# A tuned attention and GLU kernel: phi = elu+1 as a minimum on VectorE in place of an add on GpSimd, a product in four tasks, smaller first loads and a smaller last store

## The chip, the cores and the metric

The kernel runs on one core of a Trainium2 chip. The metric is the device time of one execution in microseconds, the median of several runs. A profiled execution of the same kernel gives the trace; its times are measured from the start of the profiled span. Engines are PE (TensorE), DVE (VectorE), ACT (ScalarE), POOL (GpSimd) and SP (SyncE, which here issues DMAs).

## What is computed

x has 2048 rows of 512. Two branches share it, and a gate per row mixes them:

```
phi = lambda t: jnp.where(t > 0, t + 1.0, jnp.exp(t))
for s in range(N):                       # 4 segments of 512 rows, 32 heads of 16
    p = softmax(qs @ ks.T * scale + causal mask)
    a_dot = p @ vs
    a_mem = (phi(qs) @ M) / (phi(qs) @ z + 1e-6)
    o = g * a_mem + (1 - g) * a_dot      # g = sigmoid(beta), one per head
    M = M + phi(ks).T @ vs ; z = z + sum(phi(ks))
a = o @ wo
b = (gelu(x @ w_gate) * (x @ w_up)) @ w_down      # inner width 1792
out = g_row * a + (1 - g_row) * b        # g_row = sigmoid(x . gate_w)
```

phi(t) is elu(t) + 1. It can also be had as min(exp(t), 1) + max(t, 0), or as min(exp(t), max(t, 0) + 1).

## The kernel before, in words

Everything stays on the chip between loads and stores. PSUM has eight banks of 128x512 fp32, given out one at a time ("gen") or as pairs.

The program is written as tasks, each with an engine (or a choice of two), a cost in ns, dependences, a priority, and the banks and ring buffers that it takes and frees. `Sched.plan` simulates all engines with these costs and picks, engine by engine, the ready task of lowest priority number that can start first; `Sched.emit` then issues the instructions in that order. A random term of width SPREAD from the generator SEED is added to TensorE priorities, so SEED and SPREAD alter the whole order. The order in each engine's queue is fixed once the program is built: at run time an instruction waits for what it needs, and what stands behind it on its engine waits too. Tasks with `port=True`, and all tasks of POOL, are kept from overlapping in the plan.

**Opening** (`first_k`, L523 to L573). NWARM matmuls on zeros (L529) keep TensorE busy while x arrives. Rows 0 to 511 of x come as two DMAs of 256 KB, one issued by SP and one by ACT (L395), wk likewise (L397); the other weights follow on SP (L382 to L407), then the loads of the other segments of x, transposed by DMA (L377). Sixteen matmuls against the identity (L548), four for each block `fc` of 128 columns, transpose x; DVE and ACT in turn copy each block to xT (L552, through the helper at L314 and L316); then k is computed for all columns (L562), four matmuls for each `fc`. q, v and the gate projections follow (L475, full 128x128 tiles).

**Attention** runs from about 67 us. Each segment has 20 logit slots (L731): each computes two pairs of banks with row-tiled matmuls, ACT exponentiates them (L753), POOL zeroes the upper triangle of the diagonal blocks (L762), and after each five slots the P·V products follow (L781), whose results DVE transposes (L799), normalises (L809 to L817), joins with the memory part (L822) and transposes back into xT (L825). Between slots, as fillers, stand the dense products in column tiles (L479): q, k and v of the next segment, the up projections (evicted by DVE, L653), the memory products, and the down and output projections of the segment before. NUPS says how many of the 56 up projections each segment gets.

**phi** (L838 to L859) is done for two column groups at a time, 128x1024, twice per segment for k of segments 0 to 2 and for q of segments 1 to 3: twelve times. ACT writes E = exp(t) (L843), DVE writes Q = max(t, 0) (L847) and caps E at 1 in place (L850), and POOL adds the two (L854) into pkT or pq. pkT is transposed by a DMA issued on SP (L881), for the update of M (L892).

**M** is accumulated in Macc (L906, L908). At the end of each of the segments 0 to 2, `f_mbd` (L914) writes it as a block diagonal into Mbd with four products of 32 partitions, one task of 1000 ns in the plan; zbd (L920) likewise for z. The memory products of the next segment (L964) read Mbd.

**Output** (`out_group`, L999): for each 128 rows, 14 down and 4 output quads (four column tiles each) accumulate in one bank; DVE or ACT scales it into an osb buffer (two of them), and SP stores 128 KB (L997). The four groups of the last segment come last.

Of the kernel before, what the change touches and what calls it, by code (L numbers as in the profile page):

```python
# [9 lines left out]
AF = mybir.ActivationFunctionType  # L10
# [25 lines left out]
PORTPEN = 0  # L36
NWARM = 7
NUPS = (26, 12, 10, 8)
ATT = 5
SEED = 6  # L40
SPREAD = 3.0
SHAPES = {"gen": [(b,) for b in range(NBANK)],
# [246 lines left out]
def kernel(  # L289
# [22 lines left out]
    def copy(e, dst, src):  # L312
        if e == "ACT":
            nc.scalar.activation(dst, src, AF.Copy)  # L314
        else:
# [7 lines left out]
             "pkT": 1, "pk": 2, "T": 2, "r": 2, "N": 2, "rm": 1, "Tm": 1, "Nm": 3,  # L323
             "osb": 2, "tt": 1}
    S = Sched(RINGS)
# [67 lines left out]
    x0r = x2[0:L, :].rearrange("(kt p) d -> p kt d", p=P)  # L393
    for h, eng in enumerate((nc.sync, nc.scalar)):
        eng.dma_start(xn[:, 2 * h:2 * h + 2, :], x0r[:, 2 * h:2 * h + 2, :])  # L395
    for h, eng in enumerate((nc.sync, nc.scalar)):
        eng.dma_start(wk[:, 2 * h:2 * h + 2, :], wkr[:, 2 * h:2 * h + 2, :])  # L397
    load_w(nc.sync, wq, A_wq)
# [12 lines left out]

    a_xn = ext(3600)
    a_x = [None, ext(18000), ext(22000), ext(26000)]
    a_wk, a_wq = ext(3800), ext(5500)
    a_wg0, a_wv, a_wga, a_gw, a_be, a_wup, a_wo = [ext(t) for t in (8500, 10000, 14000, 27000,
# [85 lines left out]
    def qk_group(s, c, which, prio, engs):  # L501
        pr = c // 2
        W, aw = (wk, a_wk) if which == "k" else (wq, a_wq)
        key = (which, s, pr)
        name = which + "T"

        def mk():
            QK[key] = rtile(name, [P, 2, L])
        new = key not in first_ev
        g, box = group(which, 4 * MM, lambda t: mm_x(t[:, :], W, c * P, s), prio,  # L510
                       [a_x[s], aw] + ([] if new else [first_ev[key]]),
                       also=(name, mk) if new else None)
        first_ev.setdefault(key, g)
        read_x[s].append(g)

        def fn(e, t):
            copy(e, QK[key][:, c % 2, :], t[:, :])
        ev = evac(engs, g, box, fn)
        EVQK[(which, s, c)] = ev
        if which == "k":  # L520
            odd_copy(s, c, ev)

    def first_k():  # L523
# [8 lines left out]
        add("EXT", 0, lambda _: None, deps=[w], frees=[("pair", w)])  # L532

        def f_open(_):
            for i in range(2):
                tl["x", i] = pair(op, 0)[:, i, :]
                tl["x", 2 + i] = pair(op, 1)[:, i, :]
            for i in range(2):
                tl["k", i] = pair(op, 2 + i)
                QK[("k", 0, i)] = rtile("kT", [P, 2, L])  # L540
        op = add("PE", 1, f_open, prio=-2000, deps=[w], alloc=["pair", "pair", "pair", "pair", "kT",
                                                          "kT"])
        xe = []
        prev = op
        for fc in range(FC):
            def f_t(_, fc=fc):
                for kt in range(KT):
                    nc.tensor.matmul(tl["x", fc][:, kt * P:(kt + 1) * P],  # L548
                                     lhsT=xn[:, kt, fc * P:(fc + 1) * P], rhs=ident,
                                     start=True, stop=True)  # L550
            prev = add("PE", 430, f_t, prio=-1999, deps=[prev, a_xn])
            xe.append(add("ACT" if fc % 2 else "DVE", 600,  # L552
                          lambda e, fc=fc: copy(e, xT[:, fc, 0:L], tl["x", fc]), prio=0,
                          deps=[prev], frees=[(("pair", fc // 2), op)]))
        a_x[0] = xe[-1]
        TAB["wdn"] = add("SP", 600, lambda _: load_w(nc.sync, wdn, B_w_down), deps=[prev],
                         lat=40000)
        last = None
        for fc in range(FC):
            def fn(_, fc=fc):  # L560
                for c in range(NCH):
                    nc.tensor.matmul(tl["k", c // 2][:, c % 2, :],  # L562
                                     lhsT=wk[:, fc, c * P:(c + 1) * P], rhs=xT[:, fc, 0:L],
                                     start=(fc == 0), stop=(fc == FC - 1))
            last = add("PE", 4 * MM, fn, prio=-1998, deps=[last, xe[fc], a_wk])
            read_x[0].append(last)
# [271 lines left out]
    def phi(src, deps, prio, mk, ring):  # L838
        box = {}

        def f_e(_):
            box["E"] = rtile("E", [P, 2, L])
            nc.scalar.activation(box["E"][:, :, :], src()[:, :, :], AF.Exp)  # L843

        def f_q(_):
            box["Q"] = rtile("Q1", [P, 2, L])
            nc.vector.tensor_scalar_max(box["Q"][:, :, :], src()[:, :, :], 0.0)  # L847

        def f_m(_):
            nc.vector.tensor_scalar_min(box["E"][:, :, :], box["E"][:, :, :], 1.0)  # L850

        def f_a(_):
            d = mk()
            nc.gpsimd.tensor_add(d[:, :, :], box["E"][:, :, :], box["Q"][:, :, :])  # L854
        e = add("ACT", 960, f_e, prio=prio, deps=deps + [TAB["first_x"], opened], alloc=["E"])
        q = add("DVE", 325, f_q, port=True, prio=5, deps=[e], alloc=["Q1"])
        m = add("DVE", 330, f_m, port=True, prio=5, deps=[e])
        return add("POOL", 2090, f_a, prio=5, deps=[m, q], alloc=[ring],
                   frees=[("E", e), ("Q1", q)])  # L859
# [24 lines left out]
    def m_update(s, pr, prio):  # L884

        def mms(t):
            for i in range(2):
                for kt in range(KT):
                    for j in range(4):
# [8 lines left out]
                       [PKD[(s, pr)]] + [EVV[(s, kt)] for kt in range(KT)]  # L898
                       + ([TAB[("mbd", s - 1)], TAB[("zbd", s - 1)]] if s else []),
                       frees=[("pk", PKD[(s, pr)])])  # L900
# [12 lines left out]

        def f_mbd(_):  # L914
            for j in range(4):
                a, hh = slice(32 * j, 32 * j + 32), slice(2 * j, 2 * j + 2)
                nc.vector.tensor_mul(Mbd[a, :, hh, :], Macc[a, :, :, 0:DH], bdeb[a, :, hh, :])  # L917

# [7 lines left out]
        deps = [TAB[("acc", s, 0)], acc, t_eb] + [TAB[("num", s, c)] for c in range(NCH) if s]  # L926
        TAB[("mbd", s)] = add("DVE", 1000, f_mbd, port=True, prio=3, deps=deps)
        TAB[("zbd", s)] = add("DVE", 125, f_zbd, port=True, prio=3, deps=deps + ([TAB[("den", s)]] if s else []))
# [33 lines left out]
    def mem_num(s, c, prio):  # L962
        def mms(t):
# [3 lines left out]
        g, box = group("num", MM, mms, prio,  # L967
                       [TAB[("mbd", s - 1)], TAB[("den", s)], PHI[("q", s, c // 2)]],
                       also=("Tm", lambda: bx.update(T=rtile("Tm", [P, QB, 2, DH], F32))),
# [14 lines left out]

    def down(t, s, qt, lo, hi, stop):
        for hs in range(lo, hi):
            dense(t, G[:, s, hs, qt * P:(qt + 1) * P], wdn[:, hs, :], hs == 0,
                  stop and hs == HS - 1)

    def proj_o(t, s, qt, cs, first):  # L990
        for c in cs:
            dense(t, xT[:, c, s * L + qt * P:s * L + (qt + 1) * P], wo[:, c, :],
                  first and c == 0, c == NCH - 1)

    def store(s, qt, osb):
        q0 = s * L + qt * P
        nc.sync.dma_start(out2[q0:q0 + P, :], osb[:, :])  # L997

    def out_group(s, qt, prio):  # L999


        late = s == NSEG - 1
        att = [t_wo] + [OTT[(s, c)] for c in range(NCH)]
        prev = first = None
        for lo in range(0, HS, 2):
            def fn(_, lo=lo):
                down(bank(first), s, qt, lo, lo + 2, False)
            prev = add("PE", 2 * MM, fn, prio=prio, mode="more" if lo else "open",
                       deps=[prev] if lo else [UPT[(s, hs)] for hs in range(HS)] + [TAB["wdn"]]
                       + ([] if late else att[:ATT]), alloc=[] if lo else ["gen"], final=late)  # L1010
            first = first or prev
        g = add("PE", 4 * MM, lambda _: proj_o(bank(first), s, qt, range(NCH), False),
                prio=prio, deps=[prev] + att, final=late, mode="more")
        bx = {}

        def fo(e):
            bx["o"] = rtile("osb", [P, D])
            f = omz[:, s, qt:qt + 1]
            if e == "ACT":
                nc.scalar.activation(bx["o"][:, :], bank(first), AF.Copy, scale=f)  # L1020
            else:
                nc.vector.tensor_scalar_mul(bx["o"][:, :], bank(first), f)
        ev = add(["DVE", "ACT"], [660, 585], fo, deps=[g, TAB["omz"]], alloc=["osb"],
                 frees=[("gen", first)])
        add("SP", 600, lambda _: store(s, qt, bx["o"]), deps=[ev], frees=[("osb", ev)], lat=2000)

# [34 lines left out]
    for s in range(NSEG):  # L1061
        for t in range(NSLOT):
# [7 lines left out]
            if w == 4:  # L1070
                pv_group(s, c, 0)
                pv_group(s, c, 1)
    for qt in range(KT):
        out_group(NSEG - 1, qt, 9000 + qt)

    S.plan()
# [28 lines left out]
```

## Time and profile before

| what | us |
|---|---|
| median of 3 runs (lowest to highest) | 277.24 (277.02 to 277.30) |
| the profiled execution: its time | 277.76 |
| the profiled execution: its span | 275.93 |
| POOL's adds of phi, L854, 12 of them, each | 2.13 to 2.56 |
| POOL's selects L762: 96 of 128x512, 64 of 128x256, mean each | 0.67, 0.44 |
| DVE's cap L850, 12 of them, mean | 0.45 |
| ACT's exp of logits L753, 160 of them, mean (sum) | 1.03 (154.3) |
| stores of 128 KB, median from issue to landing | 2.1 |

The span is the time from the first to the last instruction in the trace; the execution's own time has some 1.8 us around it. A row of the timeline reads: start, duration, engine, line, operation, output<-inputs, shape, how many were merged, and in brackets how long the engine stood idle before and what released it. "128\*32" after PE is the active rows and columns of the array. A row of groups has busy time, the mean in ns, and the idle time before. A row of waits has the total in us, how many, and the longest. TensorE's matmuls are pipelined: a row of 0.38 us for a 128x512 matmul overlaps the next one, which starts 0.216 us later.

### The profile page before, as it was taken

How to read it: one execution, taken by the hardware profiler on the slowest of the kernel's cores; microseconds unless marked ns; L12 is line 12 of the kernel's file. 1: busy time of each engine (PE TensorE's matmuls, PEld its weight loads, DVE VectorE, ACT ScalarE, POOL GpSimd, SP SyncE). 2: the span in 40 equal slices, each digit the busy share in tenths (PEclk: the TensorE clock that was granted, in tenths of full speed). 3: DMA queues.
4: the chain of work that ended last, by engine and by line, in shares of the span. 5: the costliest groups of instructions: out<-in, count | busy, mean ns of one | idle time of the engine just before them, and what ended most of it. 6: DMA issues, size and time to landing. Idle time of an engine off the chain costs nothing.

```text
span 275.9 us, 10157 instructions
## 1 busy us (share of the span) xinstructions
PE 268.7 (97%) x4504; PEld 125.1 (45%) x4504; DVE 173.5 (63%) x323; ACT 211.6 (77%) x233; POOL 128.9 (47%) x221
## 2 busy tenths in 40 slices
PE   8999999999999979999999999999999999999994
PEld 4444444444444434544444444544444544444451
DVE  3340003001879898869778869999976795996240
ACT  3445555556987858799889799999988999999711
POOL 8100000070477356456844776676755457564500
PEclk9999999999999999999999999999999999999999
DMA  7963890000022000200110011020000000000002
GB/s 234 355 135 77 293 315 2 0 0 2 2 44 40 2 2 2 40 2 2 21 43 23 21 22 41 2 40 6 21 21 21 21 4 4 21 21 21 24 12 67
DMA packets 22036, 14.02 MB, mean 51 GB/s; under 512 B 14056, under 2 KB 20968, under 8 KB 21992
## 3 DMA queue, kind: packets, MB, share of 16 engines
q1 hardware_dynamic: 21448, 12.85, 16.8%
q8 instruction: 35, 0.57, 0.9%
q10 hardware_dynamic: 544, 0.52, 0.6%
q14 instruction: 9, 0.07, 0.1%
HBM read 8.13 MB, written 2.10 MB: 37 GB/s over the span
## 4 chain that ended last, share of the span: by engine, by line
PE 92%; DVE 4%; ACT 1%; issue 1%; ACTq 0%
PE ps L479 53%; PE ps L475 20%; PE ps L731 9%; PE ps L781 6%; PE ps L562 1%; PE ps L529 1%; DVE G L653 1%; ACT pT L753 1%; DVE Mbd L917 1%; PE ps L548 1%; DVE vz_82 L316 0%; DVE kT L316 0%; PE ps L892 0%; PE ps L597 0%; DVE E L850 0%
## 5 line engine op out<-in xcount | busy, mean ns | idle before, releaser
L753 ACT ACTIVATE pT<-ps 128x1024 bf16<-128x1024 f32 x160 | 154.3, 1029 | 15.4 <-PE ps L731 14.7
L762 POOL TENSOR_SCALAR_AFFINE_SELECT pT<-pT 128x512 bf16<-128x512 bf16 (+1 forms) x160 | 91.6, 579 | 80.4 <-ACT pT L753 80.0
L479 PE MATMUL ps<-wdn,G 128*32 128x512 bf16 x896 | 58.5, 380 | 0.0
L479 PE MATMUL ps<-xT,wup 128*32 128x512 bf16 x896 | 55.4, 380 | 0.1
L653 DVE TENSOR_TENSOR G<-ps,G 128x512 bf16<-128x512 f32 x56 | 37.9, 681 | 21.5 <-PE ps L479 21.4
L475 PE MATMUL ps<-xT,wga 128*128 128x512 bf16 x224 | 48.9, 379 | 0.0
L643 ACT ACTIVATE G<-ps 128x1024 bf16<-128x1024 f32 x28 | 28.7, 1024 | 23.5 <-PE ps L475 23.5
L799 DVE STREAM_TRANSPOSE T<-ps 128x512 f32<-128x512 f32 x32 | 22.7, 711 | 18.6 <-PE ps L781 15.1
L475 PEld LDWEIGHTS <-wga 128*128 128x128 bf16 x224 | 21.8, 98 | 26.4 <-issue 0.4
L479 PEld LDWEIGHTS <-wup 128*32 128x32 bf16 x896 | 22.3, 96 | 22.4 <-issue 4.0
L479 PEld LDWEIGHTS <-G 128*32 128x32 bf16 x896 | 21.4, 96 | 20.0 <-issue 2.7
L614 POOL COPY G_87<-tt 32x16 f32<-32x16 f32 x16 | 3.1, 195 | 48.2 <-DVE tt L606 47.6
L731 PE MATMUL ps<-qT,kO 32*128 32x128 bf16 (+2 forms) x320 | 17.9, 272 | 0.2 <-ACT pT L753 0.2
L731 PE MATMUL ps<-qT,kT 16*128 16x256 bf16 (+2 forms) x320 | 17.6, 274 | 0.0
L479 PEld LDWEIGHTS <-xT 128*32 128x32 bf16 x448 | 11.4, 96 | 12.6 <-issue 2.8
L479 PE MATMUL ps<-wo,xT 128*32 128x512 bf16 x256 | 16.3, 380 | 0.0
L731 PEld LDWEIGHTS <-kT 16*128 16x128 bf16 x320 | 6.8, 92 | 19.6 <-issue 19.5
L817 DVE TENSOR_TENSOR N<-T,r 128x512 bf16<-128x512 f32 x16 | 14.3, 893 | 0.3
L479 PE MATMUL ps<-wv,xT 128*32 128x512 bf16 x192 | 12.3, 380 | 1.6 <-DVE G L653 1.6
L731 PEld LDWEIGHTS <-kO 32*128 32x128 bf16 x320 | 7.1, 92 | 12.3 <-issue 12.1
L1020 ACT ACTIVATE osb<-ps,omz 128x512 bf16<-128x512 f32 x8 | 5.5, 689 | 9.3 <-PE ps L479 7.6
L479 PE MATMUL ps<-xT,wq 128*32 128x512 bf16 x192 | 12.3, 380 | 0.1
(117 smaller groups left out, 276.9 us busy)
## 6 DMA issues: line engine op xcount, KB each, us to landing
out_dram<-osb SPq DMA_DIRECT2D x16, 128.0 KB, 2.1
wup<-in_B_w_up_dram SPq DMA_DIRECT2D x1, 1792.0 KB, 8.2
wdn<-in_B_w_down_dram SPq DMA_DIRECT2D x1, 1792.0 KB, 13.7
wga<-in_B_w_gate_dram SPq DMA_DIRECT2D x1, 1280.0 KB, 10.9
wq<-in_A_wq_dram SPq DMA_DIRECT2D x1, 512.0 KB, 6.2
wga<-in_B_w_gate_dram SPq DMA_DIRECT2D x1, 512.0 KB
wv<-in_A_wv_dram SPq DMA_DIRECT2D x1, 512.0 KB, 8.2
wo<-in_A_wo_dram SPq DMA_DIRECT2D x1, 512.0 KB, 9.3
```

What stands on the lines that cost most here:

```text
L475: nc.tensor.matmul(t, lhsT=lhsT, rhs=rhs, start=start, stop=stop)
L479: nc.tensor.matmul(t[a, :], lhsT=lhsT[:, a], rhs=rhs, start=start, stop=stop, tile_position=(0, 32 * j), skip_group_check=True)
L614: nc.gpsimd.tensor_copy(G2[dst, s, :], z[src, :, 0])
L643: ge = evac("ACT", g, box, lambda e, t: nc.scalar.activation(dst, t[:, :, :], AF.Gelu_apprx_tanh), cost=920, ring="pair")
L653: UPT[(s, hs)] = evac("DVE", g, box, lambda e, t: nc.vector.tensor_mul(G[:, s, hs, :], t[:, :], G[:, s, hs, :]))
L731: nc.tensor.matmul(A[j // 2][:, j % 2, at * P:(at + nq) * P], lhsT=l, rhs=r, start=True, stop=True, tile_position=(32 * j, 0))
L753: nc.scalar.activation(pT[(s, t, h)][:, :, :], A[h][:, :, :], AF.Exp, scale=0.25)
L762: nc.gpsimd.affine_select(out=v, in_=v, pattern=pat, compare_op=ALU.is_ge, fill=0.0, base=0, channel_multiplier=-1)
L781: nc.tensor.matmul(t[32 * j:32 * j + 32, qb * P:(qb + nq) * P], lhsT=vz[s % 2][:, kt, h * VW:h * VW + 32], rhs=pT[(s, t0 + w, j // 2)][:, ...
L799: nc.vector.transpose(TT[key][:, e, :, :].rearrange("p a b -> p (a b)"), t[:, :])
L817: nc.vector.tensor_mul(NN[key][:, :, :, :].rearrange("p a e d -> p e a d"), TT[key][:, :, :, 0:DH], RR[key][:, :, :, :].to_broadcast((P, 2 ...
L1020: nc.scalar.activation(bx["o"][:, :], bank(first), AF.Copy, scale=f)
```

## The change

Settings: NWARM 7 to 6; NUPS (26, 12, 10, 8) to (28, 10, 9, 9); SEED 6 to 1; SPREAD 3.0 to 1.5; ring osb from 2 to 3 buffers.

phi: the cap of E and POOL's add go; max(t, 0) + 1 is one VectorE instruction, and VectorE takes the minimum of it and E.

```diff
-            nc.vector.tensor_scalar_max(box["Q"][:, :, :], src()[:, :, :], 0.0)
-        def f_m(_):
-            nc.vector.tensor_scalar_min(box["E"][:, :, :], box["E"][:, :, :], 1.0)
+            nc.vector.tensor_scalar(out=box["Q"][:, :, :], in0=src()[:, :, :], scalar1=0.0,
+                                    scalar2=1.0, op0=ALU.max, op1=ALU.add)
         def f_a(_):
-            d = mk()
-            nc.gpsimd.tensor_add(d[:, :, :], box["E"][:, :, :], box["Q"][:, :, :])
+            nc.vector.tensor_tensor(mk()[:, :, :], box["E"][:, :, :], box["Q"][:, :, :],
+                                    op=ALU.min)
-        m = add("DVE", 330, f_m, port=True, prio=5, deps=[e])
-        return add("POOL", 2090, f_a, prio=5, deps=[m, q], alloc=[ring],
+        return add("DVE", 602, f_a, port=True, prio=5, deps=[q], alloc=[ring],
```

Mbd: four tasks of 240 ns in place of one of 1000, between which the plan may put other work; who read Mbd waits for all four.

```diff
-        def f_mbd(_):
-            for j in range(4):
-                a, hh = slice(32 * j, 32 * j + 32), slice(2 * j, 2 * j + 2)
-                nc.vector.tensor_mul(Mbd[a, :, hh, :], Macc[a, :, :, 0:DH], bdeb[a, :, hh, :])
+        def f_mbd(j):
+            a, hh = slice(32 * j, 32 * j + 32), slice(2 * j, 2 * j + 2)
+            return lambda _: nc.vector.tensor_mul(Mbd[a, :, hh, :], Macc[a, :, :, 0:DH],
+                                                  bdeb[a, :, hh, :])
...
-        TAB[("mbd", s)] = add("DVE", 1000, f_mbd, port=True, prio=3, deps=deps)
+        TAB[("mbd", s)] = [add("DVE", 240, f_mbd(j), port=True, prio=3, deps=deps)
+                           for j in range(4)]
```

Opening: four DMAs of 128 KB each for x and for wk, in turn from SP and ACT. The transposes go by halves of the rows (the first half needs the first two x loads) and by pairs of column blocks; the copies to xT have the same shape of 512 elements, DVE for the first pair of blocks and ACT for the second; k's matmuls of one `fc` need both halves.

```diff
-    for h, eng in enumerate((nc.sync, nc.scalar)):
-        eng.dma_start(xn[:, 2 * h:2 * h + 2, :], x0r[:, 2 * h:2 * h + 2, :])
+    for i in range(KT):
+        (nc.scalar if i % 2 else nc.sync).dma_start(xn[:, i, :], x0r[:, i, :])
...
-            last = add("PE", 4 * MM, fn, prio=-1998, deps=[last, xe[fc], a_wk])
+            last = add("PE", 4 * MM, fn, prio=-1998,
+                       deps=[last, xe[0, fc // 2], xe[1, fc // 2], a_wk[fc]])
```

End: `out_group` takes a slice of columns; the last 128 rows are done as two groups of 256 columns, each with its own bank, eviction and store of 64 KB.

```diff
-    for qt in range(KT):
+    for qt in range(KT - 1):
         out_group(NSEG - 1, qt, 9000 + qt)
+    for h in range(2):
+        out_group(NSEG - 1, KT - 1, 9010 + h, slice(h * D // 2, (h + 1) * D // 2))
```

In the built program TensorE has 4575 matmuls in place of 4504 (72 more because the last group is halved in columns, one warm one less), and still 80 blocks of row-tiled logits. VectorE has the 12 minima in place of the 12 caps; POOL has no phi operation left. ScalarE does 8 copies of k and of q (6 each before) and 2 of v (5 before).

## The prediction

> **What bounds the kernel now.** I read the head of the page first, then TensorE's waits, then the places in order of time where TensorE stood still, then the opening and the end. The page's head:
>
> ```profile
> span 275.9 us, 10157 instructions
> PE 268.7 (97%) x4504; PEld 125.1 (45%) x4504; DVE 173.5 (63%) x323; ACT 211.6 (77%) x233; POOL 128.9 (47%) x221
> ```
>
> TensorE (PE) is the bound, but 97% hides how much could be won. Counting the matmuls by shape and giving each its start-to-start distance (a full 128x512 matmul 216 ns; four column or row tiles of 512 together 216 ns; narrower ones in proportion), all columns take 244.4 us. TensorE works from 1.26 to 272 us, 270.7 us. The rest, from the starts of consecutive blocks: 80 blocks of row-tiled logits (L731) between column-tiled work cost 109 ns on the way out and 117 ns on the way in, together 18 us; the half-clock opening costs 3 us; and some 4.3 us are true stalls, of which TensorE's waits show the largest:
>
> ```profile
> PE ps L479 <- DVE G L653: 1.6, 1, 1.6
> PE ps L529 <- DVE wdn L392: 1.3, 1, 1.3
> PE ps L731 <- ACT pT L753: 0.2, 1, 0.2
> ```
>
> The others (0.45 us at 106, 0.29 at 117, 0.18 at 172, 0.25 at 193, 0.26 at 254, none of the rest over 0.15) hide inside busy rows, since a matmul's row lasts beyond the start of the next. Around the 1.6 us wait the timeline of VectorE (DVE), GpSimd (POOL) and TensorE shows the cause:
>
> ```profile
> 95.28 0.68 DVE L653 TENSOR_TENSOR G<-ps,G 128x512 bf16<-128x512 f32 x1
> 95.88 3.23 DVE L917 TENSOR_TENSOR Mbd<-Macc,bdeb 32x128 bf16<-32x128 f32 x4
> 99.14 1.29 DVE L653 TENSOR_TENSOR G<-ps,G 128x512 bf16<-128x512 f32 x2
> ...
> 95.96 2.19 POOL L854 TENSOR_TENSOR pq<-E,Q_1235 128x1024 bf16<-128x1024 bf16 x1
> ...
> 100.49 0.83 PE L479 MATMUL ps<-wv,xT 128*32 128x512 bf16 x12 [1.58 <-DVE G L653]
> ```
>
> The add of phi starts on POOL after the first of the four Mbd products; the second then lasts 2.13 us instead of 0.27 (all twelve):
>
> ```profile
> L917 DVE TENSOR_TENSOR Mbd<-Macc,bdeb x12: 271/286/2126, 95.9 to 198.3; 32x128 bf16<-32x128 f32 x12
> ```
>
> Behind Mbd stand two evictions L653, and the banks they free are what TensorE waits for. The opening and the end:
>
> ```profile
> 4.24 1.99 PE L548 MATMUL ps<-wdn 128*128 128x128 bf16 x16
> 6.03 1.22 PE L562 MATMUL ps<-xT,wk 128*128 128x512 bf16 x3
> ...
> 270.91 1.04 PE L479 MATMUL ps<-wo,xT 128*32 128x512 bf16 x16
> ...
> 272.05 0.69 ACT L1020 ACTIVATE osb<-ps,omz 128x512 bf16<-128x512 f32 x1 [0.92 <-PE ps L479]
> ```
>
> Transposes begin when x lands (its two issues at 0.81 land at 4.19 and 4.51), TensorE's clock row turns to full at 6.84, and after the last matmul come one eviction, a store (issued 272.76, landed 274.45) and 1.5 us of closing.
>
> **The change, part by part.**
>
> *phi.* Removed per phi, twelve times: POOL's add (2.13 us) and the cap of E on VectorE (L850, mean 0.45). The max that remains (L847, 0.36 to 0.42) gains a second scalar operation, at the same price between its own bounds. Added: a minimum of two bf16 SBUF tensors, 128x1024. No row has it; the nearest is L822, an add of two bf16 SBUF tensors at 128x512: fastest 0.38 us, mean 0.57. Doubling the elements puts the undisturbed minimum between 0.65 (only the streaming part doubles) and 0.76; I take 0.70. The Trainium skill speaks against counting GpSimd's absence as the end of the clash (SBUF — State Buffer, "Who interferes with whom"): a VectorE instruction with two SBUF inputs contends with a GpSimd one that reads SBUF, and the loser is blocked for the winner's whole instruction. POOL keeps its 160 selects (L762, 0.44 and 0.67 us). By the rule each minimum could meet a whole select, 12 x 0.67 = 8 us on VectorE; by the row L822 loses 0.19 on average, 12 x 0.19 = 2.2 us. I take the row. VectorE then gains 12 x (0.70 + 0.19 - 0.45) = 5.3 us. Against it, rows of VectorE that lie over an add exceed the fastest of their line by 8.2 us in sum (L917 1.9, L493 1.9 at 170.6, L817 1.3 at 181.3 and 1.7 at 191.0 the largest), which go. Net about -3 us of 173, and above all no single block longer than a select. The new waiting instruction is the minimum itself, behind ACT's exp; L850 stood behind the same exp and was never idle before it. Behind it queue PSUM evictions, as behind L850. phi's own chain gets shorter (2.1 us add to 0.7), which no TensorE wait of before needed.
>
> What it is worth on TensorE: the 1.8 us stall at 98.9 goes. Of the 0.45 at 106 (kT and its exp late after that block), the 0.18 at 172 and the 0.25 at 193, which all follow within 9 us of a block by an add, I count 0.7. Sum 2.5; bounds 1.3 (the next eviction in line is late anyway for 0.5) and 3.5.
>
> *Mbd in four tasks.* Same four products, same 0.29 each. In the built order one eviction now stands between them at two of three places. Three of the four collisions above don't involve Mbd, so alone it is worth little; beside the add's removal nothing: 0.
>
> *Order.* Seed, spread and up-groups per segment (28, 10, 9, 9) reshuffle everything. I set TensorE's work per segment (columns and switches, from the built order) against ScalarE's (40 exps at 0.945 us start to start, E 0.95, copies 0.49, osb 0.58). Third segment: before 44.6 to 42.2, after 42.7 to 40.7. Fourth: 41.1 to 39.9, after 40.6 to 39.0. ScalarE remains under TensorE in each, as close as before; the count of switches stays at 80 pairs. I take 0, with -0.8 to +1.5 for the bounds, since a new order can place a late eviction anywhere.
>
> *Opening.* Four x loads of 128 KB: SP and ACT issue 0.5 us apart, so wk, wq and what follows on SP are issued 1 us later. They stay hidden: wq landed at 8.06 and its first matmul is at 9.89; bytes, not issues, set these landings (some 350 GB/s from 4 us on). ACT's table load moves from 1.86 to about 2.9 and ends 4.2, before its first copy. x0 and x1 should land near 3.5, x2 and x3 near 4.2. Six warm matmuls (427 ns) end at 3.82. Transposes run from 3.82 to 5.53 at 107 ns. But k's first matmul needs the copies of *both* halves: the third group of four ends near 5.1, its copy runs 5.42 to 6.11 (0.32 and 0.69 as in the row at 4.99), and k starts near 6.25 instead of 6.03, with TensorE idle 0.7 us before. If the clock still turns at 6.84, 0.59 us at half speed replace 0.81: k ends 0.11 later. +0.1, bounds -0.2 and +0.4.
>
> *End.* The last group in two column halves: its last eviction has 256 columns. ACT's 128x1024 exp takes 1.03 and the 128x512 copy 0.69, so 256 columns cost about 0.52: -0.17. The store halves; the packets of a lone one stream for about 0.5 us of its 1.69, so -0.12 (bounds 0 and -0.25). The extra 72 quarter tiles stream 256 columns in the same total; the 128x256 tiles of L781 show no extra per tile (20 matmuls in 0.55, columns alone 0.53). A third osb buffer removes the 1.65 us ACT waits at 270.45, which TensorE doesn't feel. VectorE's last chain ends 3.3 us after the last P·V; 20 instead of 18 down quads (4.3 us) cover it. Sum -0.3.
>
> Total: -2.5 + 0.1 - 0.3 = -2.7. The profiled execution took 277.76 (span 275.93 and 1.83 around it); the median is 277.24, so 0.52 lower. Predicted span 273.2, profiled time 275.1, median 274.5.
>
> **The rivals.**
>
> *A, the blocks go, likeliest:* 274.5, its own range 273.2 to 275.8.
>
> *B, the clock comes late.* The skill (TensorE: Matmul & The Clock Gate, "What's actually happening") lets the clock open after a busy window of about 3.4 us, and the window runs freely. Before, TensorE was busy without a break from 1.26 to 6.84; the change breaks this by 0.7 us ahead of k. If the window that contains the break doesn't count, full clock comes up to 3.4 us later; at half speed that loses 1.7 us. Time 276.2. Against it: the rest of the window is busy.
>
> *C, the order gives it back.* Stalls of 4.3 us are small beside 195 us of tightly interleaved work; with ScalarE at 95% of TensorE in two segments, other banks come late elsewhere. Only the end is won: 276.9 to 277.3.
>
> *D, slower: the minimum on VectorE holds up evictions.* VectorE is busy 42.7 of 50 us from 67 to 117 and 43.6 of 48 from 165 to 213. The max and minimum stand back to back, 1.1 us, over 1.7 when a select comes between, with PSUM evictions behind them; a bank free that late stops TensorE. If each of the twelve costs TensorE its added 0.44 us, that is 5.3, and the time 274.5 + 5.3 = 279.8. It decides from 0.23 us per phi on (2.7 / 12). Against it: VectorE loses more in blocks by adds than it gains, and L850 with L847 took 0.85 in the same place without a wait named.
>
> That the change doesn't do what it says: the built order has none of the twelve adds on POOL and twelve minima on VectorE, so it does.
>
> **How the numbers follow.** A 0.59, B 0.15, C 0.11, D 0.15. What the measurement can tell from no change is 0.2%, 0.55 us: under 276.7 is faster, over 277.8 slower. A and B are faster, with a sliver of C: 0.75; most of C is the same: 0.09; D and a sliver of C: 0.16. The range runs from 273.0 (A with both unknowns at their good ends leaves some 5% below) to 277.6, which leaves most of D out.
>
> **What would show it.** No VectorE row of Mbd, L817 or L493 over 1.2 us; TensorE's stalls in sum under 2.2 us; the minimum at 0.65 to 0.9 us mean; k's first matmul at 6.1 to 6.4 with an idle place before it, and the clock row at about 6.8; last eviction about 0.5 us and 3.6 us from the last matmul to the end of the span. Wrong would be: a new TensorE wait over 1 us on a VectorE eviction (D or C), or the clock row near 10 us (B).

## The result, and the profile after

The changed kernel takes 274.87 us (median of 4 runs, 274.56 to 275.50) against 277.23 (4 runs of the kernel before beside it): ratio 0.9919, 95% interval 0.9899 to 0.9939, faster by 2.4 us. The profiled execution took 274.56 with a span of 272.74. The head of the page and TensorE's waits, to be set beside those of before:

```profile
span 272.7 us, 10273 instructions
PE 266.6 (98%) x4569; PEld 127.0 (47%) x4575; DVE 171.5 (63%) x323; ACT 211.6 (78%) x234; POOL 106.2 (39%) x209
```

```profile
PE ps L529 <- DVE wdn L392: 1.3, 1, 1.3
PE ps L479 <- ACT pT L757: 0.7, 2, 0.5
PE ps L565 <- DVE xT L316: 0.6, 1, 0.6
PE ps L475 <- issue: 0.2, 1, 0.2
```

POOL is 23 us lighter, VectorE 2 us lighter, and the 1.6 us wait on L653 is gone. New are 0.6 us ahead of k (L565) and 0.5 us on an exp of the logits. The 0.2 us at L475 is a hole in the records (six of 4575 matmuls have none), not a wait. The same place in VectorE's timeline, where the Mbd products stand after the first segment:

```profile
93.19 0.69 DVE L657 TENSOR_TENSOR G<-ps,G 128x512 bf16<-128x512 f32 x1 [0.24 <-PE ps L479]
93.82 0.23 DVE L908 COPY Macc<-ps 128x68 f32<-128x68 f32 x1
94.09 1.22 DVE L918 TENSOR_TENSOR Mbd<-Macc,bdeb 32x128 bf16<-32x128 f32 x3
95.34 0.69 DVE L316 CAST vz_82<-ps 128x512 bf16<-128x512 f32 x1
```

Three products take 1.22 us; four took 3.23. The longest of all twelve is 0.63 (behind a select), where it was 2.13. Opening and end:

```profile
2.52 1.49 PE L529 MATMUL ps<-wdn 128*128 128x512 bf16 x3
3.79 1.69 PE L550 MATMUL ps<-wdn 128*128 128x128 bf16 x16
6.05 1.24 PE L565 MATMUL ps<-xT,wk 128*128 128x512 bf16 x5 [0.56 <-DVE xT L316]
...
268.97 0.61 PE L479 MATMUL ps<-wo,xT 128*32 128x256 bf16 x16
...
269.69 0.47 ACT L1017 ACTIVATE osb<-ps,omz 128x256 bf16<-128x256 f32 x1 [1.49 <-PE ps L479]
```

It helps to cut the span in three: up to q's first matmul, from there to the end of the last matmul ("the middle"), and the rest.

| kernel, us | to q | middle | rest | span |
|---|---|---|---|---|
| before | 9.89 | 262.06 | 3.98 | 275.93 |
| after | 9.50 | 260.09 | 3.15 | 272.74 |
| difference | -0.39 | -1.97 | -0.83 | -3.19 |

The middle repeats to 0.1 us: the changed kernel and the three below that share its order from q on have 260.08 to 260.11. Opening and rest vary from one execution to the next, so one profile's -0.39 and -0.83 are not what the medians show: the profiles differ by 3.2 us, the medians by 2.4. The -0.39 is the clock's: TensorE's full clock begins at 6.84 us in the profile of before, 0.81 us after k's first matmul, and at 5.12 in that of the changed kernel, ahead of k; 0.81 us at half speed are 0.4. Most experiments are therefore judged by the middle first and by the ratio second.

### The profile page after: what moved, and what is told of

It is laid out like the page before. It is cut to its first block, busy times and chain, and to the rows that moved or that the text cites. A ratio compares the mean times of both kernels' runs of the same rounds, so it can differ in the third digit from the quotient of the medians.

```text
span 272.7 us, 10273 instructions
## 1 busy us (share of the span) xinstructions
PE 266.6 (98%) x4569; PEld 127.0 (47%) x4575; DVE 171.5 (63%) x323; ACT 211.6 (78%) x234; POOL 106.2 (39%) x209
## 4 chain that ended last, share of the span: by engine, by line
PE 97%; ACT 1%; issue 1%; DVE 0%; ACTq 0%
PE ps L479 57%; PE ps L475 20%; PE ps L735 10%; PE ps L785 6%; PE ps L565 1%; PE ps L529 1%; ACT pT L757 1%; PE ps L894 1%; PE ps L550 0%; PE ps L601 0%; DVE xT L316 0%; ACT osb L1017 0%; DVE wdn L392 0%; PE ps L666 0%; ACTq L1017 0%
## 5 line engine op out<-in xcount | busy, mean ns | idle before, releaser
L766 POOL TENSOR_SCALAR_AFFINE_SELECT pT<-pT 128x512 bf16<-128x512 bf16 (+1 forms) x160 | 94.3, 592 | 104.0 <-ACT pT L757 103.2
L479 PE MATMUL ps<-wdn,G 128*32 128x512 bf16 (+1 forms) x952 | 59.1, 368 | 0.2 <-ACT pT L757 0.2
L475 PE MATMUL ps<-xT,wga 128*128 128x512 bf16 x219 | 48.4, 379 | 0.4 <-issue 0.2
L475 PEld LDWEIGHTS <-wga 128*128 128x128 bf16 x224 | 21.7, 98 | 26.4 <-issue 0.4
L479 PEld LDWEIGHTS <-wup 128*32 128x32 bf16 x896 | 23.2, 96 | 21.1 <-issue 2.1
L479 PEld LDWEIGHTS <-G 128*32 128x32 bf16 x952 | 22.4, 96 | 19.4 <-issue 4.2
L735 PE MATMUL ps<-qT,kO 32*128 32x128 bf16 (+2 forms) x320 | 17.3, 272 | 0.0
L479 PE MATMUL ps<-wo,xT 128*32 128x512 bf16 (+1 forms) x272 | 16.5, 367 | 0.0
L479 PE MATMUL ps<-xT,wk 128*32 128x512 bf16 x192 | 12.5, 380 | 0.0
L1017 ACT ACTIVATE osb<-ps,omz 128x512 bf16<-128x512 f32 (+1 forms) x8 | 5.1, 635 | 9.4 <-PE ps L479 9.4
```

The costliest lines, as they stand in the source:

```text
L475: nc.tensor.matmul(t, lhsT=lhsT, rhs=rhs, start=start, stop=stop)
L479: nc.tensor.matmul(t[a, :], lhsT=lhsT[:, a], rhs=rhs, start=start, stop=stop, tile_position=(0, 32 * j), skip_group_check=True)
L735: nc.tensor.matmul(A[j // 2][:, j % 2, at * P:(at + nq) * P], lhsT=l, rhs=r, start=True, stop=True, tile_position=(32 * j, 0))
L766: nc.gpsimd.affine_select(out=v, in_=v, pattern=pat, compare_op=ALU.is_ge, fill=0.0, base=0, channel_multiplier=-1)
L1017: nc.scalar.activation(bx["o"][:, cols], bank(first)[:, cols], AF.Copy, scale=f)
```

## The experiments

Two theories stood against each other. Mine: GpSimd's adds block VectorE, and their removal is the gain. The rival: SEED, SPREAD and NUPS gave a luckier order. To tell them apart, phi was changed without any change of order, and the order without phi.

**Phi alone, in place.** The plan sees the old costs and engines; only what is issued changes, so every other instruction keeps its place on its engine.

```diff
-            nc.vector.tensor_scalar_max(box["Q"][:, :, :], src()[:, :, :], 0.0)
+            nc.vector.tensor_scalar(out=box["Q"][:, :, :], in0=src()[:, :, :], scalar1=0.0,
+                                    scalar2=1.0, op0=ALU.max, op1=ALU.add)
-            nc.vector.tensor_scalar_min(box["E"][:, :, :], box["E"][:, :, :], 1.0)
+            pass
-            nc.gpsimd.tensor_add(d[:, :, :], box["E"][:, :, :], box["Q"][:, :, :])
+            nc.vector.tensor_tensor(d[:, :, :], box["E"][:, :, :], box["Q"][:, :, :],
+                                    op=ALU.min)
```

> The kernel before with its order kept on every engine; only phi is rewritten: max and +1 in one VectorE instruction, the cap left out, and the minimum issued by VectorE at the place where GpSimd had its add. Theory (blocks by the adds): no VectorE row of Mbd, kO or N over 1.2 us, TensorE's 1.6 us wait at 98.9 gone, its stalls in sum down from 4.3 to between 1.8 and 2.5 us, time 274.7 to 275.4. Rival (the new order, not phi, made the gain): within 0.5 us of before, 276.7 to 277.7. Rival (minima hold up evictions): above 277.8.

Measured: 275.42, ratio 0.9937 (0.9925 to 0.9949); middle 260.93, that is -1.13. VectorE's and TensorE's timelines at the place:

```profile
95.33 1.73 DVE L919 TENSOR_TENSOR Mbd<-Macc,bdeb 32x128 bf16<-32x128 f32 x4
97.09 0.69 DVE L855 TENSOR_TENSOR pq<-E,Q 128x1024 bf16<-128x1024 bf16 x1
97.70 1.28 DVE L653 TENSOR_TENSOR G<-ps,G 128x512 bf16<-128x512 f32 x2
...
99.04 1.91 PE L479 MATMUL ps<-wv,xT 128*32 128x512 bf16 x32 [0.33 <-DVE G L653]
```

Mbd takes 1.73 in place of 3.23, the minimum 0.69, and TensorE waits 0.33 in place of 1.58. That is the whole effect: the stalls at 106, 117, 172 and 193 us of before (the prediction counted the first and the last two) are there again, 1.3 to 1.5 us earlier on the clock and to within 0.01 us of their old size (0.46, 0.29, 0.18, 0.25). So they did not follow from the adds. In sum the stalls fall from 4.3 to 3.2, not to 2.5.

**Phi back in the changed kernel, in place:** the same edit the other way round, in the changed kernel's order.

> The changed kernel with its order kept, and phi as it was: max, cap and GpSimd's add, each at the place where the new instructions stand. Theory: the adds block VectorE again, some for 1 to 2 us, and TensorE's stalls rise from 2.3 to about 4 us: 276.2 to 277.2. Rival (order): within 0.5 us of the changed kernel, 274.4 to 275.4.

Measured: 285.68, ratio 1.0304 (1.0291 to 1.0318); the middle is 270.76, 10.7 us longer. Both theories expected far less. TensorE's waits:

```profile
PE ps L785 <- POOL pT L766: 4.5, 10, 0.7
PE ps L479 <- DVE G L657: 1.3, 1, 1.3
```

Ten times TensorE waits for a select. One of the places, in POOL's and TensorE's timelines:

```profile
152.04 2.14 POOL L856 TENSOR_TENSOR pkT<-E,Q 128x1024 bf16<-128x1024 bf16 x1 [1.68 <-DVE E L853]
154.13 1.64 POOL L766 TENSOR_SCALAR_AFFINE_SELECT pT<-pT 128x512 bf16<-128x512 bf16 x3
...
154.87 0.29 PE L785 MATMUL ps<-pT,vz 128*32 128x256 bf16 x2 [0.70 <-POOL pT L766]
```

The add stands ahead of the selects in POOL's queue, P·V (L785) waits for these, and TensorE's queue has nothing else before it. In the order before, which was planned with the adds, no wait of TensorE on POOL is listed at all. So this order, planned without the adds, doesn't stand them.

**The order alone:** before, with only the three constants.

```diff
-NUPS = (26, 12, 10, 8)
+NUPS = (28, 10, 9, 9)
-SEED = 6
-SPREAD = 3.0
+SEED = 1
+SPREAD = 1.5
```

> The kernel before with only SEED 1, SPREAD 1.5 and NUPS (28, 10, 9, 9): another order, with GpSimd's adds, the Mbd task in one, the old opening and the old end. Theory: the adds still block VectorE; a new order alone is worth nothing on average: 276.4 to 278.0, with rows of VectorE near 2 us. Rival (order): 274.8 to 275.6.

Measured: 278.74, ratio 1.0057 (1.0045 to 1.0070), middle 263.71: the new constants make the kernel before slower by 1.65 us in the middle. That kills the plain rival, but also leaves my range; the reverse run bears on why.

**All of the change but the order's constants** (SEED 6, SPREAD 3.0 and the old NUPS in the changed kernel).

> The changed kernel with the old SEED 6, SPREAD 3.0 and NUPS (26, 12, 10, 8), planned anew: phi as a minimum, Mbd in four tasks, new opening and end. The new order alone made the kernel before slower by 1.5 us. If the gain is phi's and the order's share is chance: 274.6 to 276.2, TensorE's stalls 2.0 to 3.7 us. If the changed kernel's constants carry part of the gain together with phi (an order fitted to the new costs): 276.0 to 277.0.

Measured: 277.32, ratio 1.0009 (0.9999 to 1.0019), middle 262.56. The change without its constants gains nothing, though phi in place, in the order planned with the old costs, gained 1.13. Neither half carries the gain alone. One reading is that constants belong to the costs with which the planner ran; the planner agrees. Its simulated time to TensorE's last matmul (plan time, nothing measured) is 268.9 us for before and 271.6 for before with the new constants, 268.4 for the changed kernel and 270.6 for it with the old ones.

**Orders that were picked and one that was not:** three copies of the changed kernel with other constants. SEED 1002 and 1194 are among the shortest by the kernel's own planner out of 1800; SEED 2 is simply the next.

```diff
-SEED = 1
+SEED = 2
```

> The changed kernel with SEED 2 in place of 1, an order that nobody picked. If a chosen order is part of the gain: from q to the last matmul 261.3 to 264, time 275.8 to 278.5. If phi, opening and end make the gain whatever the order: 260 to 260.8, time 274.5 to 275.4.

> The changed kernel with SEED 1002 and SPREAD 3.0, an order picked out of 1800 by the kernel's own planner as one of the shortest. If the planner's choice among orders carries over to the chip, the stretch from q to the last matmul is within 0.8 us of the changed kernel's 260.1: time 274.3 to 275.7. If orders differ by chance only: anywhere from 274.5 to 278.

> The changed kernel with SEED 1194, SPREAD 2.0 and NUPS (28, 11, 9, 8), another of the shortest orders by the planner. As for SEED 1002: 274.3 to 275.7 if the planner's choice carries over to the chip, else anywhere from 274.5 to 278.

Measured: SEED 2 takes 282.69, ratio 1.0200 (1.0178 to 1.0221), middle 268.01; SEED 1002 takes 274.77, 0.9913 (0.9898 to 0.9927), middle 260.22; SEED 1194 takes 275.45, 0.9945 (0.9925 to 0.9965), middle 260.68. The unpicked order loses 7.9 us in the middle with the same work; five copies move from VectorE to ScalarE, as they do with SEED 1002, which loses nothing. Its TensorE waits:

```profile
PE ps L735 <- ACT pT L757: 3.0, 5, 1.1
```

and its TensorE and ScalarE near the end, where three logit slots are left without dense work between them, so that ScalarE's exps set the pace (one of the five waits, the longest, is at 228):

```profile
257.52 0.28 PE L735 MATMUL ps<-qT,kT 16*128 16x256 bf16 x2 [0.51 <-ACT pT L757]
258.44 0.28 PE L735 MATMUL ps<-qT,kT 16*128 16x256 bf16 x2 [0.63 <-ACT pT L757]
...
259.36 0.58 PE L735 MATMUL ps<-qT,kO 32*128 32x512 bf16 x1 [0.41 <-ACT pT L757]
260.27 0.61 PE L735 MATMUL ps<-qT,kO 32*128 32x512 bf16 x2 [0.34 <-ACT pT L757]
...
255.53 7.44 ACT L757 ACTIVATE pT<-ps 128x1024 bf16<-128x1024 f32 x8 [0.29 <-PE ps L735]
```

That is not all of the loss. In the midst of these idle places TensorE's clock falls to half for 6.83 us, which happens in no other profile here between the opening and the last matmul. In these rows of two stretches the times are busy PE, PEld, DVE, ACT and POOL, then come the granted clock and DMA:

```profile
258.93:265.76 6.83, 6.00 (x64) 2.39 (x66) 1.98 (x3) 5.98 (x7) 4.26 (x8) 0.50 0.00 0
265.76:272.00 6.24, 6.24 (x143) 3.72 (x136) 3.09 (x6) 0.00 (x0) 0.00 (x0) 1.00 0.01 3
```

Of these, the 4.95 us from 260.81 on, where P·V and dense work follow, cost some 2.5 us (an estimate, half of them). All four runs of this kernel have a mean granted clock of 0.988; all others have at least 0.996.

In the two picked orders the planner's choice carries over to the chip. SEED 2 is a bad draw rather than a usual one: its plan time is 275.5 us, the longest of the SEEDs 0 to 59, whose median is 271.0 and whose shortest is SEED 1 with 268.4; SEED 1002 and 1194 have 268.3 and 268.5. No order tried beats the changed kernel by more than the scatter.

**Mbd apart, in the order before.** After the first segment only, three of the four products are issued two evictions later; the adds stay.

```diff
+            one(0)
+            if s == 0:
+                REST.append([2, lambda: [one(j) for j in range(1, 4)]])
...
+        def fu(_, t):
+            nc.vector.tensor_mul(G[:, s, hs, :], t[:, :], G[:, s, hs, :])
+            for x in REST:
+                x[0] -= 1
+                if x[0] == 0:
+                    x[1]()
```

> The kernel before with its order and GpSimd's adds, but after the first segment only the first of the four Mbd products stays in its place; the other three follow two evictions L653 later. If TensorE's 1.6 us wait at 98.9 is the block of Mbd by the add and nothing behind it, the evictions now pass: from the start of q to the last matmul 260.9 us as with phi in place (262.06 before), time 276.0 to 276.3, at an unchanged number of adds. If the prediction's 0 for the Mbd tasks holds (other work is late anyway, or the blocked products hold the next rows just as well): 261.9 to 262.2, time 277.0 to 277.4.

Measured: 276.16, ratio 0.9966 (0.9952 to 0.9979), middle 261.03: -1.03, nearly as much as phi in place. VectorE and POOL:

```profile
95.19 0.27 DVE L923 TENSOR_TENSOR Mbd<-Macc,bdeb 32x128 bf16<-32x128 f32 x1
95.55 0.69 DVE L655 TENSOR_TENSOR G<-ps,G 128x512 bf16<-128x512 f32 x1
96.48 0.69 DVE L655 TENSOR_TENSOR G<-ps,G 128x512 bf16<-128x512 f32 x1 [0.24 <-PE ps L479]
97.20 1.21 DVE L923 TENSOR_TENSOR Mbd<-Macc,bdeb 32x128 bf16<-32x128 f32 x3
...
95.27 2.18 POOL L860 TENSOR_TENSOR pq<-E,Q 128x1024 bf16<-128x1024 bf16 x1
```

Two evictions, each with PSUM as one input, run at their usual 0.69 us beside the add; the products, with two SBUF inputs, begin their second when the add is nearly done. One collision out of four made nearly the whole cost of the adds in the order before: 1.03 of 1.13 us.

**The end, both ways.** The halves alone in the kernel before, and the changed kernel without them, with all other instructions in place.

```diff
-    for qt in range(KT):
+    for qt in range(KT - 1):
         out_group(NSEG - 1, qt, 9000 + qt)
+    for h in range(2):
+        out_group(NSEG - 1, KT - 1, 9010 + h, slice(h * D // 2, (h + 1) * D // 2))
```

> The kernel before with only the last 128 rows in two column halves (osb stays at two buffers; every other instruction keeps its place). By the terms of the prediction -0.3 us: 276.9. The profile of the changed kernel has -0.8 us behind the last matmul (eviction -0.22, store -0.16, closing -0.46); if the closing belongs to the halves and is not chance, 276.4. If the shorter last eviction is hidden anyway: 277.2.

> The changed kernel with the last 128 rows in one group as before, every other instruction in its place. Theory: the last eviction 0.69 in place of 0.47 and the store's landing 1.69 in place of 1.53: +0.4 us, 275.2 to 275.4. Rival (the halves are worth nothing, since an instruction fetch of 16 KB on one of the DMA engines, seen beside the last store of the kernel with halves alone, delays the store as often): within 0.15 us of the changed kernel.

Measured: halves alone 277.01, ratio 0.9988 (0.9975 to 1.0002); without halves 274.82, 0.9922 (0.9911 to 0.9934), against the changed kernel's 0.9919. In the profiles the parts are as priced: eviction 0.47 against 0.69, issue to landing 1.53 to 1.55 in eight kernels with halves against 1.69 or 1.70 in five without, 3.46 against 3.15 us behind the last matmul. In the times nothing of it can be told, and the spans of the runs disagree: with halves alone their median is 274.75 us against 275.4 for before, without halves 273.0 against 273.0 for the changed kernel. One reason showed once: in the profile of the halves alone, the last store took 2.95 us to land. The DMA traffic of its last 4.4 us:

```profile
DMA packets 146, 0.09 MB, mean 20 GB/s; under 512 B 16, under 2 KB 144, under 8 KB 144
...
q1 hardware_dynamic: 144, 0.07, 5.9%
q8 instruction: 1, 0.02, 2.0%
q14 instruction: 1, 0.01, 0.6%
```

Beside the store's 144 packets run two instruction fetches, of 16 and 8 KB; the first lasted from 272.32 to 273.72, and eight of the store's 128 packets of 512 B started only as it ended, from 273.70 to 274.17. In the changed kernel's profile no fetch falls there. How often this happens was not measured.

**The opening, back in the changed kernel,** and the opening with only the loads as before; the order after it is kept.

```diff
-            last = add("PE", 4 * MM, fn, prio=-1998,
-                       deps=[last, xe[0, fc // 2], xe[1, fc // 2], a_wk[fc]])
+            last = add("PE", 4 * MM - 107 * (fc == FC - 1), fn, prio=-1998,
+                       deps=[last, xe[fc], a_wk])
```

> The changed kernel with the opening as it was (seven warm matmuls, x and wk in two loads each, transposes by column blocks) and everything after it in the changed kernel's order. In the profiles so far, q starts at 9.22 and 9.30 us with the old opening where the clock is full by the first k matmul, and at 9.45 and 9.50 with the new one. Theory: the new opening costs 0.2 us and this kernel takes 274.7, with q at 9.2 to 9.9 depending on where the clock turns. Rival (the new opening gains, as the two first profiles suggest with 9.50 against 9.89): 275.2 to 275.4.

> The changed kernel with x and wk loaded in two DMAs each, as before, all else the same. Theory (bytes, not the number of loads, set when wk lands, and k waits for wk): the first transposes start 0.2 to 0.5 us later, k about 0.4 us later since the second half's copies move with them, time within 0.4 us above the changed kernel: 274.9 to 275.3. Rival (small loads are worth more, transposes from 3.8 on): over 275.4.

Measured: old opening 275.13, ratio 0.9934 (0.9918 to 0.9951); big loads 274.92, 0.9937 (0.9919 to 0.9956). Neither differs from the changed kernel's 0.9919 beyond the intervals. The profiles say more: q starts at 9.11, 9.20, 9.22, 9.30, 9.69 and 9.89 us in six kernels with the old opening (mean 9.40), and at 9.45 to 9.63 in seven with the new one (mean 9.54); with big loads at 9.72. By these, small loads gain 0.2 (one profile) and the new transposes lose more than that; in sum 0.14 us are lost, less than the old opening's own scatter of 0.8. It depends on the clock: where it is full before k begins, the old opening has q at 9.11 to 9.30 and the new one at 9.45 to 9.51; where it comes later, 9.69 and 9.89 against 9.56 to 9.63.

## Why the prediction was right, point by point

The time, 274.87 against 274.5, and the sign were right; the mechanism was right in part. The term for phi, -2.5 with a lower bound of 1.3, measured -1.13 in the order before. The other 0.84 us of the middle came with the new order and the Mbd tasks, both priced at 0. So two terms were off in opposite directions, and that the sum fits is in good part luck.

- *The collision of Mbd with the add (1.8 us):* right in place and mechanism, too large. Phi in place and Mbd apart both give 1.0 to 1.1; where the stall of 1.76 us stood (the distance between two starts, less 0.216), 0.50 are left with phi in place and 0.32 with Mbd apart, and other places take back a little (0.35 at 100.88 with Mbd apart): the "next eviction in line" that the prediction kept for its lower bound.
- *The follow-on stalls (0.7 us):* wrong. "Which all follow within 9 us of a block by an add" was nearness in time, not a chain of waits. With the adds gone these stay as they were. The three other blocks on VectorE, 1.3 to 1.9 us each, cost TensorE at most 0.1 us in the middle (-1.13 without them, -1.03 with them).
- *The order (0, bounds -0.8 to +1.5):* off. With phi in place, the old order has 260.93 and the changed kernel, with the new order and Mbd in four tasks, 260.09: -0.84. The bounds were too narrow for orders as such: the same instructions take 260.1 to 268.0 in the middle. The comparison of work per segment couldn't see this; SEED 2 keeps the same up-groups per segment and loses 7.9 us, some 2.5 of them by the clock.
- *Mbd in four tasks (0):* beside the new phi no run takes it alone, so the 0 stands unshown; beside the adds it is wrong, since three products moved are worth 1.03. "Three of the four collisions above don't involve Mbd, so alone it is worth little" was wrong: the one that does is the one that counts.
- *The minimum:* 0.65 to 1.05, mean 0.73, against 0.70 + 0.19. The select's price per minimum was below the row of L822. Rows of VectorE over 1.2 us: none. VectorE fell by 2.0 us, not 3, and TensorE's stalls to 2.3 us, just over the 2.2 named.
- *Rule against row:* the Trainium skill's rule (SBUF — State Buffer, "Who interferes with whom") is borne out by the four rows of Mbd apart, as far as this case shows it: PSUM-fed evictions pass an add (eight more L653 that start under one in before take at most 0.69 us), two-SBUF-input products don't. Two inputs are not the whole condition: L493, with one SBUF tensor and one scalar per row, was blocked in before as well, for 2.18 us at 170.58. As a price, a whole select for each minimum, it would have been 8 us; the twelve minima took 1.0 us in sum above their fastest (12 x 0.73 - 12 x 0.65).
- *Opening (+0.1):* +0.14 by the means, within scatter; the -0.39 of the two profiles is the chance of the clock. "If the clock still turns at 6.84" failed: it turned at 5.12. k starts at 6.05, not 6.25, with TensorE idle 0.56 us before.
- *Rival B, a late clock:* dead. In fourteen profiles TensorE's full clock begins between 3.95 and 6.84 us; in the eight with the break ahead of k between 3.95 and 6.34. In five of the eight it is full before the break; in three it comes 0.15 to 0.28 us after k's first matmul, so these windows counted.
- *Rival C, the order gives it back:* it happens, with SEED 6 (277.32), but not in this order.
- *Rival D, minima hold up evictions:* no run shows it. In place of the adds they shorten the middle by 1.13.
- *End (-0.3):* -0.37 by the parts in the profile (eviction -0.21, landing -0.16), not separable in the times. The other -0.46 between the two profiles lies after the store's landing, where SP passes its last semaphores: 1.48 us to the end in before, in the order alone and in Mbd apart, 0.95 to 1.06 in the others. What sets it was not found. It is not tied to the change: phi in place, with the old end, has 1.06.
- *Where TensorE's time goes:* the prediction's parts (244.4, 18, 3, 4.3) add up to 269.7, not to 270.7; the 1.0 us has no name, and no term rests on it.

Without the closing the parts are -1.97, +0.14 and -0.37, together -2.20, against -2.36 between the medians. The spans agree: their median is 275.3 to 275.4 us in the sets of runs of the kernel before, and 273.0 in the changed kernel's four. What stays open is what the new order and the Mbd tasks each give of the -0.84, and whether the halves are worth anything.

## What to carry to other kernels

Find the one stall that a collision causes before counting collisions: of four blocks of VectorE of like length, one cost TensorE nearly all that was lost. In a kernel whose order comes from a planner, test an edit in place, with the old order kept, before crediting it with what a new plan gives. And search for a good order again after each change of costs: here the constants of the other kernel's order cost 1.7 to 2.5 us in the middle, a bad draw 7.9, and the edit itself was worth 1.1.

## What the runs showed that was not expected

- An order planned without GpSimd's adds loses 10.8 us when they come back. Of the waits listed for TensorE then, 5.0 us are on POOL (selects and an add) and 1.7 us on evictions by VectorE: the queue behind an add can cost more than the engine it blocks.
- The middle of 260 us repeats to 0.03 us among four kernels with one order, while single runs differ by 1 us and more. Much of that scatter lies outside the span: the changed kernel's four runs differ by 0.94 us in time and by 0.4 in span, and one run of the halves alone took 277.90 us with a span of 274.7.
- TensorE's full clock begins anywhere from 3.95 to 6.84 us after the start of the span, and moves q by up to 0.4 us, only where k's first matmuls come before it.
- The clock can fall again in mid-kernel: in SEED 2, among idle places of no more than 0.63 us each, it was at half from 258.93 to 265.76, while a single wait of 1.1 us at 228 left it full. Sparse work on TensorE cost more there than its idle time; what exactly sets it off was not tested.
